# Attention units threaded between the pieces of a feed-forward pass: gates, keys and queries one place earlier, three result buffers, marked first loads, one guard on another engine

## The chip, the cores and the metric

One core of one Trainium2 chip (trn2). The time is the device time of one execution in microseconds; the kernel is run three times and the median is quoted. Beside the times there is one profiled execution, with a time and a span of its own; every row below comes from it.

## What is computed

A gated linear attention over 4 batches, 8 heads, 768 positions and head size 48, followed by a feed-forward pass on its output:

```
f = sigmoid(f_logit)
for t in range(768):
    state = f[t] * state + outer(k[t], v[t])      # per batch and head, 48 x 48
    y[t]  = q[t] @ state
x = y as (3072, 384)
out = (relu(x @ w_in) ** 2) @ w_out               # 384 -> 2048 -> 384
```

All data is float32. The feed-forward matmuls split each operand into a high part in the matmul's own type and a low part that is the difference, and use three matmuls for each product.

## The kernel before

**Blocks, units, pieces.** The 768 positions form six blocks of 128 (all four batches, so 512 columns). In each block the eight heads make four *units* of two heads, numbered through: unit n is block n // 4. The feed-forward pass of a block runs over 16 *pieces* f of 128 hidden rows (`Moe.run`, L175): `up` (L137) makes nine matmuls into a hidden buffer `ph` (two such buffers), `square` (L148) three ScalarE passes (relu, square, cast to `gh`), `rest` (L159) one VectorE subtraction that gives `gl` and frees the hidden buffer, and `down` (L165), two pieces later, nine matmuls into three accumulators `po`. `finish` (L201) copies the three accumulators to SBUF, on ScalarE, VectorE and ScalarE, and SyncE sends each out (L211).

**The steps of a unit** are letters (`Unit.stage`, L449): L, f, k, v load; G gates (L288, ScalarE sigmoid); K keys (L291, VectorE: a scan, a product, and a *guard*, L302, a maximum over 112x8 elements kept in `low`); Q queries (L304: a reciprocal of the guard's result, a scan, a product); T transposes on TensorE (L330), N their copy; D states and S scores on TensorE (L351, L362); M mask, C states on VectorE; r, s copies on ScalarE; Y outputs on TensorE (L400); H and X the high and low parts of the output (L425, L436); g copies of some rows between tiles by DMA (L440; on GpSimd's queue for blocks 0 and 1, on SyncE's after that).

**Weights** arrive as 64-bit words and are decoded on the chip (`decode`, L85), in four steps: an absolute value on ScalarE, four VectorE operations, a ScalarE cast that gives the high part, and a VectorE subtraction that gives the low part. There are 32 half weights (piece f, input or output matrix); a load is `weights_load` (L252), which can be *marked*: VectorE first writes one word of the destination (L256), so the load can't be issued before VectorE has come that far.

**What sets the order.** TensorE, SyncE, VectorE and ScalarE run their instructions in the order in which the program issues them; GpSimd's order is left to the scheduler. The prologue is written out by hand in `FIRST` and `SECOND` (L58, L64): a letter and a number are a step of a unit; i and o load a half weight, A I c J and B O d P are the four decode steps of an input and an output weight; `busy` are TensorE transposes without use; U R E W are `up`, `square`, `rest`, `down` of block 0. The prologue computes units 0 to 7, decodes ten half weights, and runs five pieces of block 0, whose sums are kept (`keep`, L191). After that the order of blocks is 1 (16 pieces), 0 (its other 11), then 2 to 5. In block 1 the other 22 half weights are decoded: piece n takes one where n is even and two where it is odd (n up to 14; L549). `before` (L557) runs the first two steps, and for the first of two also the cast, ahead of the piece; `after` (L563) the remaining steps, between `square` and `rest`. Weight loads for piece n are marked and issued at piece n - 4.

The units of blocks 2 to 5 are threaded into the pieces by two tables: unit i starts at piece `UNIT_AT[i]` (L55), counted over all blocks, and `STAGE_AT` (L52) lists its steps as (pieces later, place in the piece, letters). Place 0 is before `up`, 0.5 between `square` and `rest`, 1 after `down`. Its last steps, Y H X g, run at the start piece of the next unit, place 1. Units at 16, 27, 43 and 59 start at the first piece of a block; a block ends with two rounds of `down` alone and `finish`.

Of the kernel before, what the change touches and what calls it, by code (L numbers as in the profile page):

```python
# [12 lines left out]
F32 = mybir.dt.float32  # L13
# [4 lines left out]
ALU = mybir.AluOpType  # L18
ET = mybir.EngineType

P = 128
# [7 lines left out]
NT = B * TB  # L29
NZ = B * NC  # L30
CZ = C + 1
ROWS = 64 + D
# [16 lines left out]

STAGE_AT = ((-3, 0, "Lv"), (0, 0, "GK"), (0, 1, "TNQ"), (1, 1, "DSrMC"), (2, 1, "s"))  # L52


UNIT_AT = (13, 16, 18, 21, 24, 27, 31, 35, 39, 43, 47, 51, 55, 59, 63, 67, 71)  # L55


FIRST = """  # L58
f0 k0 v0 G0 L1 K0 v1 Q0 busy13 T0 L2 N0 D0 G1 r0 S0 C0 K1 s0 v2 i0 M0 busy4 T1 G2 Q1 Y0 o0 N1 L3 K2
r1 D1 H0 S1 A0 B0 X0 T2 M1 v3 N2 C1 D2 i1 Q2 s1 Y1 G3 o1 C2 r2 S2 K3 H1 L4 s2 A1 X1 busy2 T3 M2 g1  # L60
N3 Q3 Y2 v4 i2 D3 I0 H2 r3 S3 o2 G4 X2 c0 M3 L5 g2 C3 J0 s3 O0 B1 busy6 Y3 v5 K4 d0 i3 H3 G5 o3 X3
busy5 T4 P0 g3 N4 Q4 A2 D4 L6 C4 r4 busy3 S4 M4 s4 v6 I1 busy3 Y4 i4
"""
SECOND = """  # L64
U0 G6 O1 o4 H4 c1 X4 L7 R0 J1 K5 U1 d1 B2 v7 E0 T5 R1 P1 W0 Q5 N5 A3 D5 E1 r5 S5 C5 G7 W1 M5 s5 K6
Y5 Q6 H5 T6 N6 X5 r6 K7 D6 g5 S6 M6 T7 C6 N7 Q7 s6 Y6 I2 r7 H6 X6 c2 D7 g6 J2 S7 B3 C7 U2 M7 s7 O2
Y7 R2 I3 H7 d2 E2 c3 X7 P2 g7 J3 A4 W2 O3 B4 U3 I4 d3 P3 c4 R3 J4 O4 U4 E3 d4 R4 W3 P4 E4 W4
"""


class Moe:
# [103 lines left out]
    def run(self, hooks):  # L175
        for n in range(len(self.fs) + LAG):
            if n < len(self.fs):
                for hook in hooks.get((n, 0), ()):
                    hook()
                f = self.fs[n]  # L180
                self.up(f)
                self.square(f)
                for hook in hooks.get((n, 0.5), ()):
                    hook()
                self.rest(f)
            if n >= LAG:
                self.down(self.fs[n - LAG])
            for hook in hooks.get((n, 1), ()):
                hook()
# [11 lines left out]
    def finish(self, dst, part=None):  # L201
        nc = self.nc
        for e in range(NJ):
            if part:
                ob = part[e]
                nc.vector.tensor_tensor(out=ob, in0=self.po[e], in1=ob, op=ALU.add)
            else:
                tag = "ob" if self.blk == 1 else f"part{e}"
                ob = self.gp.tile([P, NT], F32, tag=tag, name=f"ob{self.blk}_{e}", bufs=1)
                (nc.vector.tensor_copy if e % 2 else nc.scalar.copy)(out=ob, in_=self.po[e])  # L210
            nc.sync.dma_start(dst(e), ob)  # L211

# [9 lines left out]
def fast_path(ctx, tc, moe, ident, low, fkqT, vN, w, out):  # L222
# [36 lines left out]
    class Unit:  # L259
# [31 lines left out]
        def keys(self):  # L291

            rr = self.wk([ROWS, NZ * CZ], "rr")
            V.tensor_tensor_scan(  # L294
                out=rr[:, ::-1], data0=self.fz[:, NZ * CZ : 0 : -1], data1=dr[:, ::-1], initial=0.0,
                op0=ALU.mult, op1=ALU.add,
            )
            V.tensor_tensor(  # L298
                out=chunks(self.kt), in0=chunks(self.kt), in1=scanned(rr)[:, :, 1:], op=ALU.mult
            )  # L300
            self.pe = low[:ROWS, self.n]
            V.tensor_scalar(out=self.pe, in0=rr[:, ::CZ], scalar1=LOWEST, scalar2=None, op0=ALU.max)  # L302

        def queries(self):  # L304

# [181 lines left out]
    def step(t):  # L487

        nm = t.rstrip("0123456789")
        n = int(t[len(nm) :])
        if nm == "busy":
            for _ in range(n):
                nc.tensor.transpose(out=pw[:, 0:P], in_=ident, identity=ident)
        elif nm in ("i", "o"):  # L500
            weights_load(n, "io".index(nm))
        elif nm in "AIcJBOdP":
            i = "AIcJBOdP".index(nm) // 4
            if nm in "AB":
                decoding[n, i] = moe.decode(n, i, pro)
            next(decoding[n, i])
        elif nm == "U":
            moe.up(n)
        elif nm == "R":
            moe.square(n)  # L510
        elif nm == "E":
            moe.rest(n)
        elif nm == "W":
            moe.down(n)
        else:
            unit(n).stage(nm)
# [3 lines left out]
    with tc.manual_schedule(engines={ET.PE, ET.SP, ET.DVE, ET.Activation}):  # L520
# [28 lines left out]
        for n in range(NF - 1):  # L549
            few = range(3 * n // 2, min(3 * (n + 1) // 2, len(halves)))  # L550
            for h in few:
                if n < AHEAD:
                    weights_load(*halves[h])
                else:
                    hook(0, n - AHEAD, 0.5, lambda h=h: weights_load(*halves[h], mark=True))

            def before(few=few):  # L557
                for h, last in zip(few, (None, *few)):
                    for m in (h, h, last):
                        if m is not None:  # L560
                            next(steps[m])

            def after(few=few):  # L563
                for h in few:
                    for _ in steps[h]:
                        pass

            hook(0, n, 0, before)
            hook(0, n, 0.5, after)
        hook(0, NF - 1, 0, third)  # L570
        for i in range(len(UNIT_AT) - 1):
            un = Unit(2 * HP + i, xs, (ps_a,))
# [182 lines left out]
```

## Time and profile before

| what | us |
|---|---|
| median of 3 runs (560.84 to 563.0) | 561.27 |
| the profiled execution | 561.55 |
| its span, first to last instruction | 559.8 |
| TensorE matmuls busy | 505.9 |
| VectorE busy | 302.1 |
| ScalarE busy | 277.3 |
| GpSimd busy | 7.3 |

In the profile PE is TensorE (PEld its weight loads), DVE VectorE, ACT ScalarE, POOL GpSimd and SP SyncE. A busy share is a mean over stages: the prologue (to about 96 us), block 1 with the decoding (to about 180 us), and the rest differ in what they wait for, so the profile is to be read stage by stage. In a row of the timeline the bracket at the end is the idle time of that engine just before, and what ended it; `issue` there, or as a link of the chain, is time in which an engine waited for nothing that the profile shows.

### The profile page before, as it was taken

The page shows a single profiled execution, that of the slowest core. Times are in us where ns is not written, and L with a number is a line of the kernel's source. Part 1 is how long each engine was busy: PE and PEld are TensorE (multiplying, and loading weights), DVE is VectorE, ACT ScalarE, POOL GpSimd, SP SyncE. Part 2 cuts the span into 40 slices and gives each one's busy share as a digit, 9 for nine tenths or more (in the row PEclk, how much of TensorE's full clock was granted, in tenths as well). Part 3 has the DMA queues.
Part 4 walks back from the last instruction along what each step waited for, and adds up shares of the span by engine and source line. Part 5 has one row for each costly group of instructions (what it writes and reads, how often), then busy time and mean ns, then how long its engine had stood idle before and what let it go on. Part 6 is the DMA issues. An engine that isn't in the chain of part 4 may idle for free.

```text
span 559.8 us, 11419 instructions
## 1 busy us (share of the span) xinstructions
PE 505.9 (90%) x4869; PEld 401.7 (72%) x4869; DVE 302.1 (54%) x571; ACT 277.3 (50%) x526; POOL 7.3 (1%) x23
## 2 busy tenths in 40 slices
PE   5758769898969699999999999999999999999994
PEld 4656556677747577777878878777877877788883
DVE  6967986788894565554453464444265442111110
ACT  3434545666654555545445455555355544444341
POOL 0101000000000000000000000000000000000000
PEclk9966869999989799999999999999999999999997
DMA  8999000234640332030220230221132000100001
GB/s 235 252 264 252 9 6 6 86 111 142 194 111 20 102 74 75 11 121 2 74 73 2 75 121 5 70 74 40 54 103 64 11 11 11 57 2 0 1 0 62
DMA packets 15066, 41.71 MB, mean 74 GB/s; under 512 B 2160, under 2 KB 5232, under 8 KB 15008
## 3 DMA queue, kind: packets, MB, share of 16 engines
q1 hardware_dynamic: 14624, 40.12, 25.9%
q0 software_dynamic: 384, 0.79, 0.8%
q8 instruction: 40, 0.66, 0.5%
q14 instruction: 18, 0.15, 0.1%
HBM read 33.82 MB, written 4.72 MB: 69 GB/s over the span
## 4 chain that ended last, share of the span: by engine, by line
PE 69%; DVE 16%; ACT 7%; issue 4%; DMA 2%; SPq 0%; DVEq 0%; ACTq 0%
PE po L170 30%; PE ph L144 29%; PE ds L367 2%; DVE wa L100 2%; DVE wa L103 2%; PE py L408 2%; PE ds L356 2%; ACT w L108 2%; DVE w L110 2%; DVE rr L308 2%; DMA fkq<-in_fkqT_dram 1%; PE py L420 1%; PE pk L334 1%; ACT gh L156 1%; ACT ph L155 1%
## 5 line engine op out<-in xcount | busy, mean ns | idle before, releaser
L144 PE MATMUL ph<-x,w 128*128 128x512 f32 x864 | 226.7, 408 | 7.7 <-DVE gl L161 7.0
L144 PEld LDWEIGHTS ph<-x,w 128*128 128x128 f32 x864 | 162.8, 193 | 49.6 <-DVE gl L161 8.1
L170 PE MATMUL po<-gh,w 128*128 128x512 f32 x576 | 181.3, 396 | 0.4 <-DVE w L110 0.4
L161 DVE TENSOR_TENSOR gl<-ph,gh 128x512 fp32r<-128x512 f32 x96 | 66.2, 690 | 168.4 <-ACT gh L156 168.4
L154 ACT ACTIVATE ph<-ph 128x512 f32<-128x512 f32 x96 | 55.9, 583 | 155.7 <-PE ph L144 155.6
L170 PEld LDWEIGHTS po<-gh,w 128*128 128x128 f32 x576 | 108.1, 188 | 26.7 <-DVE w L110 0.7
L170 PE MATMUL po<-gl,w 128*128 128x512 f32 x288 | 114.4, 397 | 2.2 <-ACT w L108 1.7
L170 PEld LDWEIGHTS po<-gl,w 128*128 128x128 f32 x288 | 54.2, 188 | 16.4 <-ACT w L108 1.8
L156 ACT CAST gh<-ph 128x512 fp32r<-128x512 f32 x96 | 56.4, 587 | 3.0
L155 ACT ACTIVATE ph<-ph 128x512 f32<-128x512 f32 x96 | 55.9, 582 | 3.0
L408 PEld LDWEIGHTS py<-sc,vn 64*64 64x64 f32 (+1 forms) x768 | 25.0, 141 | 15.1 <-issue 13.3
L408 PE MATMUL py<-sc,vn 64*64 64x64 f32 (+1 forms) x768 | 29.6, 242 | 6.6 <-issue 4.7
L294 DVE TENSOR_TENSOR_SCAN rr<-fz,dr 112x520 f32<-112x520 f32 x24 | 29.6, 1234 | 9.7 <-ACT fz L289 9.5
L420 PE MATMUL py<-rx,sx 48*48 48x64 f32 (+1 forms) x352 | 27.8, 231 | 2.8 <-issue 2.7
L308 DVE TENSOR_TENSOR_SCAN rr<-fz,dz 112x520 f32<-112x520 f32 x24 | 29.8, 1242 | 0.8
L108 ACT CAST w<-wa 128x384 fp32r<-128x384 f32 x32 | 16.4, 515 | 26.4 <-DVE wa L103 26.4
L334 PE MATMUL pk<-ident,fkq 112*128 112x112 f32 x96 | 16.7, 305 | 13.3 <-DVE fkq L298 11.0
L356 PEld LDWEIGHTS ds<-vn,kn 64*64 64x64 f32 (+1 forms) x768 | 16.9, 148 | 15.4 <-issue 5.0
L420 PE MATMUL py<-fkq,sp 48*48 48x64 f32 (+1 forms) x352 | 27.2, 231 | 0.0
L356 PE MATMUL ds<-vn,kn 64*64 64x48 f32 (+1 forms) x768 | 20.3, 239 | 7.5 <-issue 3.0
L420 PEld LDWEIGHTS py<-rx,sx 48*48 48x48 f32 (+1 forms) x352 | 23.8, 141 | 3.1 <-issue 2.9
L367 PE MATMUL ds<-fkq 48*64 48x64 f32 x768 | 22.1, 250 | 3.7 <-DVE fkq L311 2.8
(56 smaller groups left out, 368.7 us busy)
## 6 DMA issues: line engine op xcount, KB each, us to landing
fkq<-in_fkqT_dram SPq DMA_DIRECT2D x23, 672.0 KB, 6.1
raw<-in_w_dram SPq DMA_DIRECT2D x32, 384.0 KB, 9.1
vn<-in_vN_dram SPq DMA_DIRECT2D x24, 192.0 KB, 5.3
out_dram<-ob SPq DMA_DIRECT2D x15, 256.0 KB, 2.0
x<-ys SPq DMA_DIRECT2D x24, 64.0 KB, 2.3
x<-ys POOLq DMA_DIRECT2D x12, 64.0 KB, 6.4
out_dram<-part SPq DMA_DIRECT2D x3, 256.0 KB, 2.1
fkq<-in_fkqT_dram SPq DMA_DIRECT2D x1, 448.0 KB, 4.1
```

Of the source, the lines that this page charges most:

```text
L144: self.nc.tensor.matmul(self.ph[f], lhsT=l, rhs=r, start=j == 0 and i == 0, stop=j == NJ - 1 and i == 2)
L154: nc.scalar.activation(ph, ph, AF.Relu)
L155: nc.scalar.activation(ph, ph, AF.Square)
L156: nc.scalar.copy(out=gh, in_=ph)
L161: self.nc.vector.tensor_tensor(out=gl, in0=self.ph.pop(f), in1=gh.bitcast(F32), op=ALU.subtract)
L170: self.nc.tensor.matmul(self.po[e], lhsT=l, rhs=r, start=f == self.fs[0] and i == 0, stop=f == self.fs[-1] and i == 2,)
L294: V.tensor_tensor_scan(out=rr[:, ::-1], data0=self.fz[:, NZ * CZ : 0 : -1], data1=dr[:, ::-1], initial=0.0, op0=ALU.mult, op1=ALU.add,)
L308: V.tensor_tensor_scan(out=pp, data0=self.fz[:, : NZ * CZ], data1=dz, initial=0.0, op0=ALU.mult, op1=ALU.add)
L356: nc.tensor.matmul(self.ds[h * C : h * C + m, c, b * D : (b + 1) * D], lhsT=self.kn[rows, b, h * C : h * C + m], rhs=self.vn[rows, b, h * ...
L367: nc.tensor.matmul(self.ds[c * C : (c + 1) * C, h, B * D + b * C : B * D + (b + 1) * C], lhsT=self.kt[rows, cs], rhs=self.ra[rows, cs], st ...
L408: nc.tensor.matmul(self.py[h * C : h * C + m, c, b * C : (b + 1) * C], lhsT=self.vn[rows, b, h * D : h * D + m], rhs=self.sc[rows, h, b], ...
L420: nc.tensor.matmul(self.py[h * C : h * C + m, c, b * C : (b + 1) * C], lhsT=s[rows, b * D : b * D + m], rhs=q[rows], start=False, stop=b = ...
```

## The change

Six edits. `STAGE_AT` moves the loads from three to four pieces ahead, G and K from place 0 of a unit's first piece to place 1 of the piece before (which is directly ahead of that piece's other hooks, and at a block's first piece ahead of the last two `down` and of `finish`), and Q from after T, at place 1, to place 0.5, between `square` and `rest`. A new place 0.7 after `rest` takes the last weight's remaining steps, so that only the subtraction of the first of two stays ahead of `rest`. `finish` uses three different buffers for its three copies: `ob`, and one each of the rotating `gh` and `gl` buffers. The guard runs on GpSimd and is issued before the product instead of after it. The prologue's ten weight loads are marked. `FIRST` and `SECOND` list the same steps in a slightly different order, with five of the 36 `busy` transposes at other places, and with the weight loads i3, o3, i4 and o4 further back.

```diff
-STAGE_AT = ((-3, 0, "Lv"), (0, 0, "GK"), (0, 1, "TNQ"), (1, 1, "DSrMC"), (2, 1, "s"))
+STAGE_AT = ((-4, 0, "Lv"), (-1, 1, "GK"), (0, 0.5, "Q"), (0, 1, "TN"), (1, 1, "DSrMC"), (2, 1, "s"))
 FIRST = """
-f0 k0 v0 G0 L1 K0 v1 Q0 busy13 T0 L2 N0 D0 G1 r0 S0 C0 K1 s0 v2 i0 M0 busy4 T1 G2 Q1 Y0 o0 N1 L3 K2
-r1 D1 H0 S1 A0 B0 X0 T2 M1 v3 N2 C1 D2 i1 Q2 s1 Y1 G3 o1 C2 r2 S2 K3 H1 L4 s2 A1 X1 busy2 T3 M2 g1
-N3 Q3 Y2 v4 i2 D3 I0 H2 r3 S3 o2 G4 X2 c0 M3 L5 g2 C3 J0 s3 O0 B1 busy6 Y3 v5 K4 d0 i3 H3 G5 o3 X3
-busy5 T4 P0 g3 N4 Q4 A2 D4 L6 C4 r4 busy3 S4 M4 s4 v6 I1 busy3 Y4 i4
+f0 k0 v0 G0 L1 K0 v1 Q0 busy13 T0 L2 N0 D0 G1 S0 C0 r0 K1 s0 v2 i0 M0 busy4 T1 Q1 G2 Y0 o0 N1 K2 r1
+D1 L3 H0 S1 A0 X0 T2 B0 M1 C1 N2 v3 Q2 D2 s1 i1 Y1 G3 C2 o1 r2 K3 S2 s2 H1 L4 A1 X1 T3 M2 g1 N3 Q3
+Y2 v4 i2 D3 I0 H2 r3 S3 G4 X2 c0 M3 g2 C3 L5 J0 s3 O0 B1 busy6 Y3 o2 K4 d0 v5 H3 X3 busy5 T4 G5 P0
+g3 i3 N4 Q4 A2 busy3 D4 L6 C4 r4 busy2 S4 M4 s4 I1 busy3 Y4 v6
 SECOND = """
-U0 G6 O1 o4 H4 c1 X4 L7 R0 J1 K5 U1 d1 B2 v7 E0 T5 R1 P1 W0 Q5 N5 A3 D5 E1 r5 S5 C5 G7 W1 M5 s5 K6
-Y5 Q6 H5 T6 N6 X5 r6 K7 D6 g5 S6 M6 T7 C6 N7 Q7 s6 Y6 I2 r7 H6 X6 c2 D7 g6 J2 S7 B3 C7 U2 M7 s7 O2
+U0 H4 O1 c1 G6 X4 R0 J1 L7 K5 U1 d1 B2 E0 T5 R1 P1 W0 Q5 v7 N5 A3 D5 E1 r5 S5 C5 G7 W1 M5 s5 o3 K6
+Y5 Q6 T6 H5 N6 X5 r6 K7 D6 g5 S6 M6 T7 C6 N7 i4 o4 Q7 s6 Y6 I2 r7 H6 X6 c2 D7 g6 J2 S7 B3 C7 U2 M7
...
@@ Moe.run
                 self.rest(f)
+                for hook in hooks.get((n, 0.7), ()):
+                    hook()
@@ Moe.finish
-                tag = "ob" if self.blk == 1 else f"part{e}"
-                ob = self.gp.tile([P, NT], F32, tag=tag, name=f"ob{self.blk}_{e}", bufs=1)
+                tag, bufs = (("ob", 1), ("gh", None), ("gl", None))[e]
+                ob = self.gp.tile([P, NT], F32, tag=tag, name=f"ob{self.blk}_{e}", bufs=bufs)
@@ Unit.keys, after the scan
+            self.pe = low[:ROWS, self.n]
+            G.tensor_scalar(out=self.pe, in0=rr[:, ::CZ], scalar1=LOWEST, scalar2=None, op0=ALU.max)
             V.tensor_tensor(
                 out=chunks(self.kt), in0=chunks(self.kt), in1=scanned(rr)[:, :, 1:], op=ALU.mult
             )
-            self.pe = low[:ROWS, self.n]
-            V.tensor_scalar(out=self.pe, in0=rr[:, ::CZ], scalar1=LOWEST, scalar2=None, op0=ALU.max)
@@ step
-            weights_load(n, "io".index(nm))
+            weights_load(n, "io".index(nm), mark=True)
@@ hooks of the decoding
-            def after(few=few):
+            def after(few=few[:-1]):
                 for h in few:
+                    next(steps[h])
+
+            def last(few=few):
+                for h in few[-1:]:
                     for _ in steps[h]:
                         pass
             hook(0, n, 0, before)
             hook(0, n, 0.5, after)
+            hook(0, n, 0.7, last)
```

## Rows read from the trace of the kernel before

**Rows 1.** Table of stages: busy us (x instructions) of PE, PEld, DVE, ACT, POOL; clock; DMA.

```profile
98.00:154.00 56.00, 50.25 (x210) 38.60 (x208) 47.23 (x116) 36.49 (x73) 0.00 (x0) 1.00 0.44 134
154.00:172.00 18.00, 12.62 (x108) 9.60 (x107) 15.86 (x32) 10.24 (x21) 0.00 (x0) 0.91 0.37 85
172.00:194.00 22.00, 17.74 (x188) 13.99 (x187) 8.34 (x15) 8.44 (x16) 0.00 (x0) 0.84 0.25 77
...
240.00:480.00 240.00, 237.19 (x2387) 189.14 (x2387) 111.95 (x191) 122.01 (x229) 0.00 (x0) 1.00 0.19 53
```

**Rows 2.** Chain of waits in the first 100 us: start us, us, what.

```profile
26.49 4.04 issue
...
35.76 2.71 issue
```

**Rows 3.** VectorE's timeline in the prologue: start us, us, instruction, idle before.

```profile
32.32 0.69 DVE L438 TENSOR_TENSOR x<-py,x 112x512 fp32r<-112x512 f32 x1 [2.61 <-ACT x L434]
...
55.06 0.69 DVE L161 TENSOR_TENSOR gl<-ph,gh 128x512 fp32r<-128x512 f32 x1 [1.47 <-ACT gh L156]
```

**Rows 4.** DMA from 12 to 30 us: the total and one issue line.

```profile
DMA packets 1577, 4.74 MB, mean 264 GB/s; under 512 B 212, under 2 KB 493, under 8 KB 1575
...
x<-ys POOLq DMA_DIRECT2D x4, 64.0 KB, 8.7
```

**Rows 5.** DMA from 27 to 29 us, by queue: packets, MB, share.

```profile
q8 instruction: 1, 0.02, 4.0%
```

**Rows 6.** DMA from 56 to 98 us: one issue line.

```profile
x<-ys POOLq DMA_DIRECT2D x3, 64.0 KB, 2.1
```

**Rows 7.** Timeline of the decode stretch, VectorE and TensorE.

```profile
107.92 2.36 PE L144 MATMUL ph<-x,w 128*128 128x512 f32 x9 [1.31 <-DVE gl L161]
...
119.70 0.56 DVE L110 TENSOR_TENSOR w<-wa,w 128x384 fp32r<-128x384 f32 x1 [0.58 <-ACT w L108]
...
125.48 0.56 DVE L110 TENSOR_TENSOR w<-wa,w 128x384 fp32r<-128x384 f32 x1 [0.44 <-ACT w L108]
```

**Rows 8.** Timeline around block 2's first unit, TensorE.

```profile
154.99 2.33 PE L144 MATMUL ph<-x,w 128*128 128x512 f32 x9 [0.75 <-DVE gl L161]
...
164.06 0.60 PE L334 MATMUL pk<-ident,fkq 112*128 112x112 f32 x4 [4.63 <-DVE fkq L298]
...
164.43 3.89 PE L144 MATMUL ph<-x,w 128*128 128x512 f32 x9
...
171.44 2.36 PE L144 MATMUL ph<-x,w 128*128 128x512 f32 x9
```

**Rows 9.** Timeline of the seam of blocks 1 and 0, TensorE and ScalarE.

```profile
179.93 2.26 PE L144 MATMUL ph<-x,w 128*128 128x512 f32 x9
...
184.38 0.59 ACT L210 COPY ob<-po 128x512 f32<-128x512 f32 x1 [5.06 <-DMA out_dram<-ob]
...
188.24 4.07 PE L144 MATMUL ph<-x,w 128*128 128x512 f32 x9
...
193.34 2.37 PE L144 MATMUL ph<-x,w 128*128 128x512 f32 x9
```

**Rows 10.** TensorE's timeline at the seam before block 2.

```profile
252.32 0.69 PE L367 MATMUL ds<-fkq 48*64 48x64 f32 x32 [0.99 <-DVE fkq L311]
```

**Rows 11.** Chain of waits, one group of a steady piece.

```profile
259.51 2.10 PE po L170 x9
```

**Rows 12.** Groups by line and shape: busy us, mean ns, idle before.

```profile
L308 DVE TENSOR_TENSOR_SCAN rr<-fz,dz 112x520 f32<-112x520 f32 x24 | 29.8, 1242 | 0.8
...
L298 DVE TENSOR_TENSOR fkq<-fkq,rr 112x512 f32<-112x512 f32 x24 | 16.6, 692 | 0.8
...
L302 DVE TENSOR_SCALAR low<-rr 112x8 f32<-112x8 f32 x24 | 3.9, 164 | 0.0
...
L240 POOL TENSOR_SCALAR_AFFINE_SELECT mask<-mask 64x64 f32<-64x64 f32 x2 | 0.5, 234 | 0.1
```

**Rows 13.** The page's DMA issues: us from issue to landing.

```profile
out_dram<-ob SPq DMA_DIRECT2D x15, 256.0 KB, 2.0
```

More of the change, by code (lines that the diff above doesn't have):

```diff
@@ L48 @@
 ORDER = (3, 0, 1, 2)
-STAGE_AT = ((-3, 0, "Lv"), (0, 0, "GK"), (0, 1, "TNQ"), (1, 1, "DSrMC"), (2, 1, "s"))
+STAGE_AT = ((-4, 0, "Lv"), (-1, 1, "GK"), (0, 0.5, "Q"), (0, 1, "TN"), (1, 1, "DSrMC"), (2, 1, "s"))
 UNIT_AT = (13, 16, 18, 21, 24, 27, 31, 35, 39, 43, 47, 51, 55, 59, 63, 67, 71)
 FIRST = """
-f0 k0 v0 G0 L1 K0 v1 Q0 busy13 T0 L2 N0 D0 G1 r0 S0 C0 K1 s0 v2 i0 M0 busy4 T1 G2 Q1 Y0 o0 N1 L3 K2
-r1 D1 H0 S1 A0 B0 X0 T2 M1 v3 N2 C1 D2 i1 Q2 s1 Y1 G3 o1 C2 r2 S2 K3 H1 L4 s2 A1 X1 busy2 T3 M2 g1
-N3 Q3 Y2 v4 i2 D3 I0 H2 r3 S3 o2 G4 X2 c0 M3 L5 g2 C3 J0 s3 O0 B1 busy6 Y3 v5 K4 d0 i3 H3 G5 o3 X3
-busy5 T4 P0 g3 N4 Q4 A2 D4 L6 C4 r4 busy3 S4 M4 s4 v6 I1 busy3 Y4 i4
+f0 k0 v0 G0 L1 K0 v1 Q0 busy13 T0 L2 N0 D0 G1 S0 C0 r0 K1 s0 v2 i0 M0 busy4 T1 Q1 G2 Y0 o0 N1 K2 r1
+D1 L3 H0 S1 A0 X0 T2 B0 M1 C1 N2 v3 Q2 D2 s1 i1 Y1 G3 C2 o1 r2 K3 S2 s2 H1 L4 A1 X1 T3 M2 g1 N3 Q3
+Y2 v4 i2 D3 I0 H2 r3 S3 G4 X2 c0 M3 g2 C3 L5 J0 s3 O0 B1 busy6 Y3 o2 K4 d0 v5 H3 X3 busy5 T4 G5 P0
+g3 i3 N4 Q4 A2 busy3 D4 L6 C4 r4 busy2 S4 M4 s4 I1 busy3 Y4 v6
 """
 SECOND = """
-U0 G6 O1 o4 H4 c1 X4 L7 R0 J1 K5 U1 d1 B2 v7 E0 T5 R1 P1 W0 Q5 N5 A3 D5 E1 r5 S5 C5 G7 W1 M5 s5 K6
-Y5 Q6 H5 T6 N6 X5 r6 K7 D6 g5 S6 M6 T7 C6 N7 Q7 s6 Y6 I2 r7 H6 X6 c2 D7 g6 J2 S7 B3 C7 U2 M7 s7 O2
-Y7 R2 I3 H7 d2 E2 c3 X7 P2 g7 J3 A4 W2 O3 B4 U3 I4 d3 P3 c4 R3 J4 O4 U4 E3 d4 R4 W3 P4 E4 W4
+U0 H4 O1 c1 G6 X4 R0 J1 L7 K5 U1 d1 B2 E0 T5 R1 P1 W0 Q5 v7 N5 A3 D5 E1 r5 S5 C5 G7 W1 M5 s5 o3 K6
+Y5 Q6 T6 H5 N6 X5 r6 K7 D6 g5 S6 M6 T7 C6 N7 i4 o4 Q7 s6 Y6 I2 r7 H6 X6 c2 D7 g6 J2 S7 B3 C7 U2 M7
+s7 O2 Y7 R2 I3 H7 d2 E2 c3 X7 P2 g7 J3 A4 W2 O3 B4 U3 I4 d3 P3 c4 R3 J4 O4 U4 E3 d4 R4 W3 P4 E4 W4
 """
```

## Prediction, made before any run of the change

> **What bounds the kernel now.** I read the table of stages first, then the chain of waits stage by stage, then each engine's order of instructions around the links where the chain leaves TensorE. From 240 to 480 us TensorE is busy 237.2 of 240 us [rows 1]: a piece is two groups of nine matmuls of 2.10 us each [rows 11], 4.2 us, and only idle TensorE time can be won there. Three earlier stages are another matter: in 98:154 it idles 5.75 us, in 154:172 5.4 us, in 172:194 4.3 us, and in the last two the granted clock falls to means of 0.91 and 0.84 [rows 1]. Before 98 us look for what makes VectorE wait: there it runs almost without gaps.
>
> **Prologue (up to 96 us).** The chain has two links in which TensorE waits for nothing that the profile shows, 4.04 and 2.71 us, both within a unit's output matmuls [rows 2]. One packet of the instruction queue moves within 27 to 29 us [rows 5]: I take the first link for TensorE's instructions arriving late, and the second for the same. VectorE pays: it waits 2.61 us for the cast behind the first link [rows 3]. A 64 KB transfer between two tiles, issued on another queue, lands in a median of 8.7 us in this stretch [rows 4] and in 2.1 us after 56 us, with the engines nearly idle [rows 6]; so a small transfer loses about 6.6 us to the full queues. The change gives ten weight loads a marker written by VectorE, so SyncE can't issue them, nor any load behind them, until VectorE gets there. My sum: without the first link the cast comes before VectorE has finished the four decode operations ahead of it, so the 2.61 us go. Without the second the next such cast comes in time too; I count 0.9 us, a third of the link. The first hidden-layer group follows the last of these outputs, where VectorE waits 1.47 us for its cast [rows 3]; I count 0.7 us, half of it. Together 4.2 us. It can be 0 (the instructions still come late) or, with second link and last wait in full, 2.6 + 2.7 + 1.5 = 6.8 us.
>
> The held-back loads put waits on SyncE. Behind the first two markers is the fourth unit's 672 KB load. The second marker is written after the second unit's queries, some 16 us in; weights and load are 1056 KB, at the 264 GB/s of rows 4 some 4 us, and with the 2.1 us of a quiet small transfer they land near 22 us. VectorE wants that unit's gates at 22.5 us. I count 0; the ends are 0 and 4 us, should the load take the 8.7 us of the crowded queue. The marker is a memset of one word; bounded by the guard's 164 ns [rows 12], ten cost 0 to 1.6 us of VectorE. I take 0.6.
>
> **Guard on GpSimd.** It removes 24 instructions of 164 ns from VectorE [rows 12]; the next instruction starts before such a one has ended, so I count 0.07 us each, 0.6 us in the prologue's eight, which pays for the markers. GpSimd has no such instruction in the trace; its nearest row is a select of 64x64 elements at 234 ns [rows 12]. The guard starts beside the product of 692 ns that follows the scan, and would end before it; so 0. Only two units ask for queries straight after keys (the first, which then waits for a load anyway, and the seventh). Ends: 0 and, for the nine units of the stretches that VectorE bounds, 0.3 us each, 2.7 us. GpSimd's queue also holds the tile-to-tile transfers of the first two blocks, which wait for a unit's lower part; VectorE's order puts that part ahead of every guard written after it, so no guard waits for a later VectorE step. *The Trainium skill speaks against this edit*: GPSIMD Engine Reference, Key points, says that GpSimd shares its SBUF interfaces with VectorE and contends with VectorE instructions that have two SBUF inputs. The product is one. By that rule the guard would end after the product and the sum come out up to 2.7 us higher; no row here has the two engines side by side.
>
> **Decode stretch of block 1 (97 to 155 us).** Two pieces carry three weight decodes. Five such periods lie between the up-projections at 107.92 [rows 7] and 154.99 us [rows 8], 9.41 us each. In each, VectorE waits 0.58 and 0.44 us for ScalarE's cast of a weight [rows 7], and TensorE starts an up-projection late (1.31 us the first time [rows 7]) because `rest`, which frees its buffer, stands behind the last weight's subtraction. The edit puts `rest` ahead. Then VectorE does `rest` while ScalarE makes the cast, and both waits go: 9.41 - 1.02 = 8.39 us for VectorE, 8.4 for TensorE's four groups. Two engines at the same load don't mesh perfectly: I take 8.47, a gain of 0.94 per period, 4.7 us. The up-projection at 107.92 itself starts about its 1.31 us earlier by the same swap. Together 6.0 us; ends 0 and the 5.75 us idle plus a quarter microsecond of restart per period, 7.0.
>
> **First unit of block 2 (155 to 180 us).** Keys stand behind eight weight operations and TensorE waits 4.63 us for their product at its transposes; the next nine matmuls then take 3.89 us instead of about 2.1 [rows 8]: the clock is at its lower level, 1.2 GHz, after that wait. Now gates and keys come before piece 13's decodes, and queries between them and `rest`. VectorE stays the limit. From `rest` of piece 11 to that of piece 13 it has three decodes with subtractions, two `rest`, keys and queries. The first two items are one period's 8.4 us; keys and queries are each a scan of 1.24 and a product of 0.69 [rows 12], with a reciprocal of about 0.2: 4.1 us, so 12.5 us; and since up-projection 15 also needs the last subtraction, 13.2 us. Before, the distance was 16.45 us (154.99 to 171.44 [rows 8]). Gain 3.3 us; ends 1.5 (clock loss stays) and 5.5 (TensorE's own 10 us and one wait). TensorE's idle time there is cut in two smaller pieces.
>
> **Seam of blocks 1 and 0 (180 to 193 us).** All three result copies use one buffer, so ScalarE waits 5.06 us for transfers to land [rows 9], VectorE likewise, and behind ScalarE's wait stand the next unit's gates, then its keys, then TensorE's transposes: 4.26 us idle [rows 1], and the next nine matmuls take 4.07 us [rows 9]. Three buffers remove both waits, and gates and keys come before the copies as well. From the first up-projection (179.93) to the third (193.34) [rows 9] are 13.4 us; without waits there remain 3.4 us to the end of the previous unit's outputs, transposes 0.6 [rows 8], the second up-projection 2.1, state and score matmuls about 1.1: 7.2. Gain 6.2 us, ends 4.3 and 6.5. The borrowed `gh` and `gl` buffers are wanted again by the third piece of the next block, at least 4.2 us later, when a result has landed (2.0 us [rows 13]); if that cover failed, it would cost some 2 us at each seam.
>
> **Seams of later blocks.** Three times scores wait for queries, 0.99 us the first time [rows 10], and restart with 2.37 instead of 2.10 us for nine matmuls [rows 9, 11]; in 240:480 the idle time is 2.8 us [rows 1]. Queries now precede `rest` of the piece before, with ScalarE's three passes as cover: 2.8 + 3 x 0.27 = 3.6 us; ends 2 and 3.6. What waits behind them is that `rest`, wanted only two pieces on. In the steady pieces these moves cost 0. Loads go out four pieces ahead instead of three, so SyncE issues each one piece earlier and the cover before the gates grows to four pieces of 4.2 us.
>
> **Sum.** 4.2 + 6.0 + 3.3 + 6.2 + 3.6 = 23.3, less 0.3 for small things left over: 23.0 us. The profiled execution took 561.55 us (span 559.8 and 1.75 around it), 0.28 above the median of 561.27. Forecast 538.5 us.
>
> **Rivals.** *Holding loads back gives nothing* (the two links are not late instructions, or the loads only crowd the next ones): 542.7 us. For it: the profile names no cause at either link; against: the packet in the same stretch, and 8.7 against 2.1 us. The Trainium skill, Runtime: NRT & Kernel Launch, Instruction fetch mechanics, has the next block of instructions fetched while the current one executes, at a cost mostly hidden; by that rule this rival holds. *The decode stretch keeps its period*, because another in-order wait takes the place (ScalarE's weight cast ahead of its own relu): 544.5 us. Against it: ScalarE is busy 36.5 of 56 us [rows 1]. *The guard contends* and doesn't leave VectorE alone, so that part of the change doesn't do what it says: 541.2 us. *Slower*: held-back loads become the prologue's limit. Five units' loads stand behind markers; if each took 8.7 us or more and, with weights ahead of it, came 5 us after its cover ends, 25 us, that would make 563.5 us. It decides itself at the fourth unit's gates: if they run after 27 us rather than near 22, this is under way. Against: most of what crowds the queue is what is being held back.
>
> **Chances.** Forecast 0.58, no gain from loads 0.16, decode period kept 0.13, contention 0.06, slower 0.04, and 0.03 that gains and losses cancel. A measurement of this kernel can't tell less than about 0.5% (2.8 us) from no change: faster 0.93, same 0.03, slower 0.04. Range: upward to the decode rival with 2.5 us of another part missing, 547; downward, prologue (2.6 more), first unit (2.2 more) and decode (1.0 more) at their ends, not quite all at once: 533.5.
>
> **What would show it.** In the profile after: no idle TensorE time over 2 us between 25 and 40 us; a decode period near 8.5 us with no VectorE wait for a weight cast; no 4 us idle where 164 and 187 us were, and a granted clock of 1.00 there; results copied without waiting for a transfer; scores at later seams not waiting for queries. I am wrong if the period stays at 9.4 us, or if ScalarE's gates wait for loads beyond the third unit.

## The result and the profile after

The changed kernel takes 536.09 us (median of four executions, 535.00 to 538.29) against 561.13 us (four, 560.84 to 563.00): ratio 0.955, 95% interval 0.951 to 0.959. The forecast was 538.5 us with a range from 533.5 to 547. The profiled execution is the slowest of the four, 538.29 us with a span of 536.6.

The table of stages of the kernel after, columns as in [rows 1]:

```profile
98.00:154.00 56.00, 53.80 (x232) 42.50 (x231) 52.98 (x126) 39.21 (x78) 0.99 (x1) 1.00 0.51 161
154.00:172.00 18.00, 17.20 (x193) 13.43 (x192) 15.41 (x29) 12.53 (x25) 0.74 (x1) 1.00 0.12 45
172.00:194.00 22.00, 21.92 (x272) 17.41 (x271) 14.05 (x24) 13.96 (x28) 1.11 (x2) 1.00 0.35 88
240.00:480.00 240.00, 239.47 (x2280) 191.41 (x2280) 103.55 (x168) 122.19 (x227) 7.40 (x10) 1.00 0.17 46
```

The idle TensorE time of the four stretches fell from 5.75, 5.4, 4.3 and 2.8 us to 2.2, 0.8, 0.1 and 0.5, and the granted clock is 1.00 in all four. In 98:154 VectorE is now busy 52.98 of 56 us and TensorE 53.80. From piece 4 to piece 13 TensorE sets the pace: it has no idle time between 105 and 147 us, and its up-projections start every 4.20 us ((147.01 - 109.22) / 9), the time of a steady piece. VectorE's own period is only just shorter (experiment 9).

TensorE's timeline of the kernel after (answers to [rows 7 to 9]; start, duration, instruction, idle before):

```profile
94.64 4.36 PE L144 MATMUL ph<-x,w 128*128 128x512 f32 x18
...
104.93 2.36 PE L144 MATMUL ph<-x,w 128*128 128x512 f32 x9 [0.93 <-DVE gl L161]
...
109.22 2.26 PE L144 MATMUL ph<-x,w 128*128 128x512 f32 x9
...
147.01 2.26 PE L144 MATMUL ph<-x,w 128*128 128x512 f32 x9
...
152.12 0.60 PE L336 MATMUL pk<-ident,fkq 112*128 112x112 f32 x4 [0.74 <-DVE fkq L302]
152.49 2.34 PE L144 MATMUL ph<-x,w 128*128 128x512 f32 x9
...
158.41 0.69 PE L369 MATMUL ds<-fkq 48*64 48x64 f32 x32 [0.59 <-DVE fkq L313]
159.03 2.58 PE L144 MATMUL ph<-x,w 128*128 128x512 f32 x9
...
167.75 2.26 PE L144 MATMUL ph<-x,w 128*128 128x512 f32 x9
...
171.40 2.36 PE L144 MATMUL ph<-x,w 128*128 128x512 f32 x9
...
174.78 1.43 PE L144 MATMUL ph<-x,w 128*128 128x512 f32 x5
```

These are up-projections: block 1 begins at 94.64 (pieces 0 and 1 in one row), piece 3 starts at 104.93, piece 4 at 109.22, piece 13 at 147.01, piece 15 at 159.03, the next block's first three at 167.75, 171.40 and 174.78 (the last row ends with the view, after five of its nine). The waits of 4.63 us ahead of the first unit's transposes [rows 8] and of 5.06 us ahead of the result copy [rows 9] are gone. From these starts and those of before (block 1 began there at 96.35) the ledger of the two profiled executions, in us:

| stretch | before | after | gain | predicted |
|---|---|---|---|---|
| up to block 1's first product | 96.35 | 94.64 | 1.7 | 4.2 |
| to up-projection 13 (decode) | 58.64 | 52.37 | 6.3 | 6.0 |
| to up-projection 15 (first unit) | 16.45 | 12.02 | 4.4 | 3.3 |
| to the next block's first | 8.49 | 8.72 | -0.2 | 0 |
| to its third (seam) | 13.41 | 7.03 | 6.4 | 6.2 |
| to the end of the span | 366.46 | 361.82 | 4.6 | 3.6 |

It adds up to 23.2 us, against 23.3 less 0.3 predicted. The term that stands out is the first. VectorE's and ScalarE's timelines of the prologue after, and two links of its chain of waits:

```profile
25.86 1.24 DVE L296 TENSOR_TENSOR_SCAN rr<-fz,dr 112x520 f32<-112x520 f32 x1 [3.58 <-ACT fz L291]
...
53.25 0.69 DVE L161 TENSOR_TENSOR gl<-ph,gh 128x512 fp32r<-128x512 f32 x1 [0.81 <-ACT gh L156]
```

```profile
25.20 0.63 ACT L291 ACTIVATE fz<-fkq 112x512 f32<-112x512 f32 x1 [4.88 <-DMA fkq<-in_fkqT_dram]
```

```profile
15.62 0.33 SPq L259
...
16.00 9.18 DMA fkq<-in_fkqT_dram
```

Both TensorE links without a cause [rows 2] are gone, and so is the VectorE wait of 2.61 us [rows 3]. In their place VectorE waits 3.58 us for the fourth unit's gates: its load went out at 16.0 us, behind the markers, and landed 9.18 us later. TensorE's timeline of the same stretch:

```profile
27.93 0.98 PE L336 MATMUL pk<-ident,fkq 112*128 112x112 f32 x4 [4.41 <-DVE fkq L302]
...
39.21 0.60 PE L336 MATMUL pk<-ident,fkq 112*128 112x112 f32 x4 [2.52 <-DVE fkq L302]
```

TensorE idles 4.41 and 2.52 us for the keys of the fourth and the fifth unit. So here the prediction's sign of being right, no idle TensorE time over 2 us between 25 and 40 us, did not come, and its sign of being wrong, gates that wait for loads beyond the third unit, did: ScalarE waits 4.88 us.

Last, the guard, in the groups by line and shape of the kernel after, beside the product it runs with:

```profile
L301 POOL TENSOR_SCALAR low<-rr 112x8 f32<-112x8 f32 x24 | 17.8, 742 | 360.3 <-DVE rr L296 360.3
```

```profile
L302 DVE TENSOR_TENSOR fkq<-fkq,rr 112x512 f32<-112x512 f32 x24 | 16.6, 692 | 0.8
```

On GpSimd the guard takes 742 ns, not the 234 ns of the nearest row; the product beside it keeps the 692 ns of before [rows 12].

### The profile page after: what moved, and what is told of

It reads as the page before. It is cut to its first block, busy times and chain, and to the rows that moved or that the text cites. A ratio compares the mean times of both kernels' runs of the same rounds, so it can differ in the third digit from the quotient of the medians.

```text
span 536.6 us, 11462 instructions
## 1 busy us (share of the span) xinstructions
PE 498.2 (93%) x4869; PEld 397.7 (74%) x4869; DVE 299.0 (56%) x557; ACT 277.3 (52%) x526; POOL 25.4 (5%) x47
## 4 chain that ended last, share of the span: by engine, by line
PE 72%; DVE 16%; ACT 5%; DMA 3%; issue 2%; SPq 0%; ACTq 0%; DVEq 0%
PE po L170 31%; PE ph L144 31%; DMA fkq<-in_fkqT_dram 3%; DVE wa L100 2%; PE ds L369 2%; PE ds L358 2%; PE py L410 2%; DVE w L110 2%; DVE gl L161 2%; DVE wa L103 2%; PE pk L336 2%; PE py L422 2%; DVE wa L99 2%; DVE rr L310 1%; ACT w L108 1%
## 5 line engine op out<-in xcount | busy, mean ns | idle before, releaser
L144 PE MATMUL ph<-x,w 128*128 128x512 f32 x864 | 223.4, 404 | 2.6 <-DVE gl L161 2.0
L301 POOL TENSOR_SCALAR low<-rr 112x8 f32<-112x8 f32 x24 | 17.8, 742 | 360.3 <-DVE rr L296 360.3
L410 PEld LDWEIGHTS py<-sc,vn 64*48 64x48 f32 (+1 forms) x768 | 24.9, 142 | 10.1 <-issue 8.3
```

The lines of the kernel that those rows point to most:

```text
L144: self.nc.tensor.matmul(self.ph[f], lhsT=l, rhs=r, start=j == 0 and i == 0, stop=j == NJ - 1 and i == 2)
L410: nc.tensor.matmul(self.py[h * C : h * C + m, c, b * C : (b + 1) * C], lhsT=self.vn[rows, b, h * D : h * D + m], rhs=self.sc[rows, h, b], ...
```

## The experiments

A single execution is read by two lengths: the start of block 1, and the **rest**, from there to the end of the span. The rest repeats: 441.96 us in the profile above, 441.86 us in the second profile of the same kernel. The table gives for each kernel the fourth unit's gates on ScalarE (the start of that sigmoid), the two lengths, and the device time: a median of four or five executions, or one execution where "(1)" stands.

| kernel | gates | block 1 | rest | us |
|---|---|---|---|---|
| before | 20.01 | 96.35 | 463.45 | 561.13 |
| after | 25.20 | 94.64 | 441.96 | 536.09 |
| after again | 22.12 | 91.34 | 441.86 | 534.86 (1) |
| without markers | 19.59 | 96.73 | 443.07 | 537.92 |
| fourth load early | 19.86 | 93.08 | 442.02 | 534.37 |
| `rest` last | 21.82 | 90.91 | 450.89 | 543.54 (1) |
| one copy buffer | 21.57 | 90.26 | 445.54 | 537.46 (1) |
| old places | 24.75 | 93.81 | 450.79 | 546.35 (1) |
| queries late | 21.74 | 90.08 | 447.62 | 539.39 (1) |
| guard on VectorE, 32 B more | 21.75 | 91.36 | 433.54 | 526.48 |
| 32 B more | 21.58 | 93.14 | 433.96 | 528.65 |
| before, 32 B more | 19.93 | 95.79 | 456.11 | 552.87 |
| guard on VectorE, 64 B more | | | | 535.16 |
| the three put together, 96 B more | 20.15 | 91.13 | 436.87 | 528.78 |

**1. The markers.** Taken from all ten loads of the prologue:

```diff
-            weights_load(n, "io".index(nm), mark=True)
+            weights_load(n, "io".index(nm))
```

> The changed kernel with the prologue's ten weight loads unmarked again; order of the lists as changed. Theory (the markers took TensorE's late instructions away, and cost the fourth unit's gates a 3.58 us wait for their load): waits without a shown cause of about 4 and 2.7 us come back on TensorE between 20 and 40 us, VectorE no longer waits for the fourth unit's gates, the first up-projection of block 1 starts near 96 us instead of 94.6; some 1.5 us slower than the changed kernel, about 537.6. Rival (the new order of the lists did it, the markers only cost): no such waits, the 3.58 us gone, start near 91 us, about 532.5 us.

537.92 us (ratio to before 0.959, interval 0.955 to 0.963, which overlaps that of the change). TensorE's timeline and then VectorE's:

```profile
30.64 0.40 PE L410 MATMUL py<-sc,vn 64*48 64x64 f32 x4 [3.96 <-issue]
```

```profile
32.42 0.69 DVE L440 TENSOR_TENSOR x<-py,x 112x512 fp32r<-112x512 f32 x1 [3.02 <-ACT x L436]
...
54.90 0.69 DVE L161 TENSOR_TENSOR gl<-ph,gh 128x512 fp32r<-128x512 f32 x1 [2.33 <-ACT gh L156]
```

The first link is back with its old size (4.04 us before) and so are the VectorE waits behind it. The DMA view of this kernel from 27 to 31 us, its total and the instruction queue:

```profile
DMA packets 217, 0.88 MB, mean 220 GB/s; under 512 B 20, under 2 KB 26, under 8 KB 216
...
q8 instruction: 1, 0.02, 2.1%
```

The queues are full during the link (SyncE's transfers alone take 95.8% of the DMA engines' time), and one packet of instructions moves, as in [rows 5]. The fourth unit's wait is gone. So the link comes of loads that go out early, and the markers do remove it: it is also there, 3.77 us, in experiment 9's kernel before, while the longest TensorE wait of that kind between 15 and 42 us in a profile with markers is 1.70 us (experiment 3). The new order of the lists alone gains nothing: without markers block 1 starts at 96.73 us (96.35 before). The second link stayed away: that one was not shown to be the markers'. In time the exchange is worth 2.1 us of block 1's start here (96.73 against 94.64) and 5.4 us against the second profile below. By the Trainium skill (Runtime: NRT & Kernel Launch, Instruction fetch mechanics) fetching is mostly hidden; at this link, if it is a fetch, it was not: 3.96 us.

**2. The fourth unit's load** put ahead of the two markers:

```diff
-... K1 s0 v2 i0 M0 busy4 T1 Q1 G2 Y0 o0 N1 K2 r1
-D1 L3 H0 ...
+... K1 s0 v2 L3 i0 M0 busy4 T1 Q1 G2 Y0 o0 N1 K2 r1
+D1 H0 ...
```

> The changed kernel with the fourth unit's load of gates, keys and queries moved ahead of the first marked weight load. Theory (that load waits only because SyncE is held by two markers in front of it, and then lands 9.2 us after issue): it lands before 17 us, VectorE's wait of 3.58 us goes, no long wait of TensorE comes back; block 1 starts near 91.2 us, about 532.8 us. Rival (the instructions come late again, as the queue is full to 17 us): a TensorE wait of 2 us or more with no shown cause between 20 and 30 us, block 1 at 93.5 us or later, 535 or more.

534.37 us (ratio 0.953, interval 0.949 to 0.956). The 3.58 us wait is gone, and block 1 begins 1.6 us earlier, not 3.4: TensorE and VectorE now wait elsewhere. Against the second profile of the kernel after (experiment 3) it even begins 1.7 us later, so the move is not shown to win; the median is 1.7 us lower, with intervals that overlap. TensorE's timeline here, VectorE's, ScalarE's, and a link of the chain of waits:

```profile
33.00 0.36 PE L422 MATMUL py<-rx,sx 48*64 48x64 f32 x1 [2.06 <-ACT sx L330]
```

```profile
32.59 0.56 DVE L110 TENSOR_TENSOR w<-wa,w 128x384 fp32r<-128x384 f32 x1 [1.63 <-ACT w L108]
```

```profile
31.52 0.63 ACT L291 ACTIVATE fz<-fkq 112x512 f32<-112x512 f32 x1 [3.29 <-DMA fkq<-in_fkqT_dram]
```

```profile
22.65 8.85 DMA fkq<-in_fkqT_dram
```

The next load behind the markers takes the place of the first: the fifth unit's goes out at 22.65 us and lands 8.85 us later, ScalarE waits 3.29 us for it, and the copy and the cast that TensorE and VectorE wait for stand behind that unit's gates in ScalarE's order. The theory had only the fourth unit's load in view; the rival's wait without a shown cause did not come either.

**3. The changed kernel once more**, one profile:

> The changed kernel once more, for one profile of another execution. Theory: the landing of the fourth unit's load behind its two markers differs between executions of one program (9.18 us after its issue in the profile shown, 5.71 and 5.91 us in the two experiments that leave this stretch alone); if it lands in under 6.5 us here, VectorE's 3.58 us wait for that unit's gates is gone, the second block starts at 90 to 91.5 us in place of 94.64, and the time is 534 to 536 us. Rival: the nine microseconds belong to this kernel's own order of issues: then the wait of 3 to 4 us is there again and the block starts near 94.6.

The link of its chain of waits:

```profile
15.68 6.41 DMA fkq<-in_fkqT_dram
```

The load lands 6.41 us after its issue, VectorE's wait shrinks from 3.58 to 0.82 us, and block 1 begins at 91.34. In the experiments that keep this stretch it took 5.71 us (`rest` last), 5.91 (one copy buffer), 5.87 (32 B more) and 8.41 (old places). The landing differs between executions of one order of issues; the profile after had the longest one. In these eight profiles with markers ahead of the load block 1 begins between 90.08 and 94.64 us, median 91.35: 5.0 us earlier than before. Where the fourth unit's gates come in time, 2 to 3 us of spread remain (93.14 with 32 B more); most of it is the fifth unit's load again, in the chain of waits of that kernel:

```profile
22.89 9.20 DMA fkq<-in_fkqT_dram
```

There ScalarE waits 3.62 us for it and starts the fifth unit's gates at 32.12. In the five other profiles whose fourth gates start by 22.2 us, the fifth start between 29.66 and 30.97 and block 1 between 90.08 and 91.36.

**4. `rest` behind the last weight again.** The cast and subtraction of the last weight go back ahead of `rest`; all else stays:

```diff
-            def after(few=few[:-1]):
+            def after(few=few):
                 for h in few:
-                    next(steps[h])
+                    for _ in steps[h]:
+                        pass
...
             hook(0, n, 0.5, after)
-            hook(0, n, 0.7, last)
```

> The changed kernel with the last weight's cast and subtraction ahead of rest again. Theory (that order alone set the decode period): the period from one up-projection to the second after it is 9.4 us again instead of 8.42, VectorE waits for ScalarE's weight cast; five periods 4.9 us and the first 1.1: some 6 us slower than the changed kernel, about 542 us. Rival (earlier gates and queries, or the lighter VectorE without guards, made the stretch faster): period under 8.8 us, less than 2.5 us slower.

The rest is 8.9 us longer, where the theory had some 6. VectorE waits for ScalarE's cast of a weight again, 0.44 and 0.58 us in every period; in the kernel after it has no such wait between 98 and 154 us. TensorE's timeline:

```profile
102.51 2.36 PE L144 MATMUL ph<-x,w 128*128 128x512 f32 x9 [1.35 <-DVE gl L161]
...
149.58 2.34 PE L144 MATMUL ph<-x,w 128*128 128x512 f32 x9 [0.74 <-DVE gl L161]
...
162.29 0.69 PE L369 MATMUL ds<-fkq 48*64 48x64 f32 x32 [1.59 <-DVE fkq L313]
162.92 3.73 PE L144 MATMUL ph<-x,w 128*128 128x512 f32 x9
```

The period is that of before, (149.58 - 102.51) / 5 = 9.41 us, and from block 1's start to up-projection 13 are 58.67 us: the whole decode gain (6.3) hangs on this edit. What the theory left out is the next stretch: 13.34 us to piece 15 in place of 12.02, then 3.73 us for nine matmuls and another 1.3 us lost.

**5. One copy buffer again:**

```diff
-                tag, bufs = (("ob", 1), ("gh", None), ("gl", None))[e]
+                tag, bufs = ("ob" if self.blk == 1 else f"part{e}"), 1
```

> The changed kernel with the result copies in the old buffers (one for block 1). Theory (early gates and keys free TensorE's transposes, buffers free ScalarE's passes): ScalarE waits about 5 us again at the seam of blocks 1 and 0, but the transposes don't; from the first to the third up-projection about 9 us instead of 7.0 (13.4 before), 2 us slower than the changed kernel, 538. Rival (the buffers are the whole of it): 13 us again and a clock at its lower level, 6 us slower, 542.

The rest is 3.6 us longer, 3.0 of it at the seam: its first three up-projections start at 163.34, 167.00 and 173.40, 10.06 us against 7.03 (13.41 before). ScalarE's timeline and TensorE's:

```profile
167.79 0.59 ACT L212 COPY ob<-po 128x512 f32<-128x512 f32 x1 [5.06 <-DVE fkq L313]
```

```profile
171.52 0.88 PE L358 MATMUL ds<-vn,kn 64*64 64x48 f32 x29 [2.17 <-ACT ph L154]
```

ScalarE loses its 5.06 us at the copy again (the releaser named had long been done; with one buffer it is again the transfer out of it that comes last), but the gates and keys are already past. With the new order of steps the buffers are worth 3.0 us at the seam (the theory had 2) and 0.6 us after it.

**6. All old places** of a unit's steps, with the marker, the buffers and the place of `rest` kept:

```diff
-STAGE_AT = ((-4, 0, "Lv"), (-1, 1, "GK"), (0, 0.5, "Q"), (0, 1, "TN"), ...
+STAGE_AT = ((-3, 0, "Lv"), (0, 0, "GK"), (0, 1, "TNQ"), ...
```

> The changed kernel with the whole old list of places (gates, keys and queries back where they stood); marker, three buffers, order of the rest and GpSimd guard stay. Theory: each early move pays at its own place. The first unit's keys product again follows one piece behind its gates, so its [rows 8] wait of some 4.6 us is back and the stretch from the last decode gate product to the next piece goes from 12.02 us to 15 to 16.5; the seam goes from 7.03 us to about 8; each of the three later seams loses 1.3 us to a waiting score product [rows 10]. Together 7.8 to 9.6 us from the start of the second block to the end, stage by stage, against the changed kernel. Rival: once the rest comes with its 0.7 hook and the copies have their buffers, the old places hide as well; then at most 3 us over the same stages.

The rest is 8.8 us longer: 4.1 at the first unit, 1.2 at the seam, 3.8 after it, 0.2 won between. TensorE's timeline:

```profile
154.91 0.80 PE L336 MATMUL pk<-ident,fkq 112*128 112x112 f32 x4 [4.36 <-DVE fkq L302]
155.38 3.79 PE L144 MATMUL ph<-x,w 128*128 128x512 f32 x9
```

The stall of [rows 8] is back, with its slow products.

**7. The queries alone** back at place 1, gates and keys still early:

```diff
-... (-1, 1, "GK"), (0, 0.5, "Q"), (0, 1, "TN"), ...
+... (-1, 1, "GK"), (0, 1, "TNQ"), ...
```

> The changed kernel with the queries alone put back on the piece's end; gates and keys stay one piece early. Theory: the gain at the later seams came from the queries' half piece (the score products no longer wait for the query copy): score products wait again some 1.0 to 1.3 us at each of three later seams and about 1 us at the first one, 4 to 6 us in all from the second block's start. Rival: the early keys made that gain; then the seams stay within 1 us of the changed kernel's and no score product waits.

The rest is 5.7 us longer: 1.1 at the first unit, 1.2 at the seam, 3.5 after it, 0.2 won between. TensorE's timeline at the first two seams:

```profile
171.75 0.69 PE L369 MATMUL ds<-fkq 48*64 48x64 f32 x32 [0.99 <-DVE fkq L313]
...
231.37 0.69 PE L369 MATMUL ds<-fkq 48*64 48x64 f32 x32 [0.99 <-DVE fkq L313]
```

The waits of [rows 10] return (0.98 us each at the other two later seams), so the gain at the later seams is the queries'; early gates and keys give the 3.0 us more at the first unit.

Experiments 4, 5 and 6 summed lengthen the rest by 8.9 + 3.6 + 8.8 = 21.3 us; the change shortened it by 463.45 - 441.96 = 21.5. Each was taken out alone, and the three together come to nearly all of it. The loads' fourth piece of lead was only taken back together with the places (experiment 6) and has no price of its own.

**8. The guard back on VectorE,** and three of the same instruction alone on GpSimd at the start (they only add work):

```diff
+    alone = pers.tile([ROWS, NZ], F32, name="alone")
+    for _ in range(3):
+        G.tensor_scalar(out=alone, in0=dr[:, ::CZ], scalar1=LOWEST, scalar2=None, op0=ALU.max)
...
-            self.pe = low[:ROWS, self.n]
-            G.tensor_scalar(out=self.pe, in0=rr[:, ::CZ], scalar1=LOWEST, scalar2=None, op0=ALU.max)
             V.tensor_tensor(
                 out=chunks(self.kt), in0=chunks(self.kt), in1=scanned(rr)[:, :, 1:], op=ALU.mult
             )
+            self.pe = low[:ROWS, self.n]
+            V.tensor_scalar(out=self.pe, in0=rr[:, ::CZ], scalar1=LOWEST, scalar2=None, op0=ALU.max)
```

> The changed kernel with the guard back on VectorE behind the product, and three extra instructions on GpSimd, of the guard's own operation and shape, at the start, before VectorE has its first two-input product. Theory (contention): beside the products the guard took 742 ns on GpSimd; alone it takes 0.2 to 0.3 us, and on VectorE 164 ns [rows 12] 24 times, which adds some 3.9 us of VectorE time that lies mostly beside the matrix products: time within 0.7 us of the changed kernel's. Rival (own cost): GpSimd takes about 0.7 us for it alone too. Second rival, for the time: the guard's 742 ns beside the product was on the path, and the kernel gains over 1 us with VectorE's guard.

The three, in the groups by line and shape of this kernel:

```profile
L255 POOL TENSOR_SCALAR alone<-dr 112x8 f32<-112x8 f32 x3 | 0.7, 236 | 0.3
```

Alone, on another tile (`dr`), it takes 236 ns, beside the product 742. That agrees with the rule of the Trainium skill that was weighed (GPSIMD Engine Reference, Key points), and GpSimd is the one that waits: the product's 692 ns did not change. But the time fell to 526.48 us (ratio 0.939, interval 0.936 to 0.942), where neither theory had it: my theory said the time of the change, and the second rival, a gain of over 1 us with no size, put it down to the guard. The groups show where from. TensorE's products of the kernel after, and then of this one:

```profile
L170 PE MATMUL po<-gh,w 128*128 128x512 f32 x576 | 181.3, 396 | 0.4 <-DVE w L110 0.4
```

```profile
L170 PE MATMUL po<-gh,w 128*128 128x512 f32 x576 | 177.4, 389 | 0.5 <-DVE w L110 0.5
```

Each product is 7 ns shorter at the same granted clock. The edit had also put a new 32-byte tile ahead of the working pools. In the built program the first input tile stands at byte 168,032 of a partition in the kernels before and after, 32 past a multiple of 64, and at 168,064 here; likewise all inputs and all `gh` and `gl`, the operands that stream through these products. The decoded weights stand at the same addresses in all these kernels. Three more kernels separate guard and address; each adds this line, a tile of 32 bytes without use, to the kernel after, to the kernel before (9) and to the kernel of experiment 8 (10):

```diff
+    pad = pers.tile([ROWS, NZ], F32, name="pad")
```

**9. The 32 bytes alone,** in the kernel after and in the kernel before:

> The changed kernel, guard on GpSimd, with one unused tile of 32 bytes per partition ahead of the working pools and nothing else. Theory (address): it moves the matrix products' moving operands (inputs x, squares gh and gl) from addresses that leave 32 when divided by 64 to addresses that leave 0; a 128x512 product of the layer takes 389 ns in the trace in place of 396, and the last steady stretch holds 134 products in 30 us in place of 130. Some 76 pieces of 18 products each lie in the stretch that TensorE bounds: 76 x 18 x 7 ns = 9.6 us less, 525 us. Rival (guard): the experiment with the guard back on VectorE won its 8.4 us because GpSimd no longer works beside VectorE; then the pad does nothing here and the time is 534 to 537 us.

> The kernel before with the same unused 32 bytes and nothing else. Theory (address): it has the same stretch of some 76 pieces, so it gains about 9 us: 550 to 553 us, products of 389 ns in the trace. Rival: its products stay at 396 ns and the time within 1 us of 560.6.

528.65 us (ratio 0.942, interval 0.938 to 0.945) and 552.87 us (0.985, 0.979 to 0.991). TensorE's up-projections in a steady stretch, of the kernel after and of the kernel after with 32 B more:

```profile
487.30 2.26 PE L144 MATMUL ph<-x,w 128*128 128x512 f32 x9
491.50 2.26 PE L144 MATMUL ph<-x,w 128*128 128x512 f32 x9
495.70 2.26 PE L144 MATMUL ph<-x,w 128*128 128x512 f32 x9
```

```profile
486.94 2.20 PE L144 MATMUL ph<-x,w 128*128 128x512 f32 x9
491.02 2.20 PE L144 MATMUL ph<-x,w 128*128 128x512 f32 x9
495.10 2.20 PE L144 MATMUL ph<-x,w 128*128 128x512 f32 x9
```

A piece takes 4.08 us in place of 4.20, 6.7 ns for each of its 18 products. The rest is 8.0 us shorter than that of after, and 7.3 us in the kernel before. The theory's 9.6 us counted the decode stretch as TensorE's; there the gain is small. Up-projections 3 and 13 of the kernel after with 32 B more:

```profile
103.37 2.35 PE L144 MATMUL ph<-x,w 128*128 128x512 f32 x9 [0.98 <-DVE gl L161]
...
145.13 2.34 PE L144 MATMUL ph<-x,w 128*128 128x512 f32 x9
```

A period takes (145.13 - 103.37) / 5 = 8.35 us in place of 8.42, where two of TensorE's pieces would take 8.16: here VectorE is the limit.

**10. The guard's place alone,** experiment 8 with a pad that restores the remainder of 32:

> The experiment with the guard back on VectorE, with another 32 bytes beside its own, so that the moving operands stand at the changed kernel's remainders of 32 again. Theory (address): this is then the guard's place alone; GpSimd's 742 ns lay beside other work and VectorE's 164 ns do too: 534 to 536.5 us and products of 396 ns. Rival (guard): the time stays near 526.5 us with the guard on VectorE, whatever the addresses.

535.16 us (ratio 0.956, interval 0.952 to 0.960), by times alone: the execution that was profiled took 2,657 us, the other four 533.87 to 538.12, and no row of that profile is used, so its products' 396 ns are not checked. With the operands where they were, the guard's place makes no difference that can be measured. With them moved, the rests differ by 0.4 us (433.54 and 433.96); the medians differ by 2.2 us, with intervals that overlap, and block 1 starts 1.8 us apart in the two profiles.

**11. Put together:** experiment 2's early load, the guard on VectorE, and a pad of 96 bytes (`ROWS, 3 * NZ`):

> The changed kernel with an unused tile of 96 bytes (the moving operands' addresses then leave 0 when divided by 64, but 64 when divided by 128), the fourth unit's load issued ahead of the markers, and the guard on VectorE. Theory: a remainder of 0 by 64 is what the products need: 389 ns each, 434 us from the second block's first product to the end of the span, and with that block starting at 91 to 93 us a time of 526 to 528 us. Rival: they need 0 by 128: then 396 ns, 442 us and 533 to 536 us.

528.78 us (ratio 0.946, interval 0.942 to 0.950), between the two theories. The steady stretch:

```profile
487.31 2.22 PE L144 MATMUL ph<-x,w 128*128 128x512 f32 x9
491.43 2.22 PE L144 MATMUL ph<-x,w 128*128 128x512 f32 x9
495.55 2.22 PE L144 MATMUL ph<-x,w 128*128 128x512 f32 x9
```

A piece takes 4.12 us, so a remainder of 0 by 64 with 64 by 128 gives most of it, and 0 by 128 the rest. Block 1 starts at 91.13 us here and at 93.08 in experiment 2, with the same order of loads; the fifth unit's gates start at 30.74 and 31.52. The best version measured is the kernel of experiment 8, 526.48 us.

## Why the prediction was right, step by step

The total was right, 536.1 for 538.5 us, and the terms behind block 1's start hold one by one. That the ledger's 23.2 us meet the forecast's 23.0 so closely is luck: 2.5 us missing in the prologue are made up by 2.1 us more at the first unit and the later seams.

- **Decode: right.** Predicted period 8.47 us, measured (147.01 - 104.93) / 5 = 8.42; VectorE no longer waits for a weight's cast. The two limits of the sum, 8.39 us for VectorE and 8.4 for TensorE, were right too: TensorE takes 8.40 from piece 4 on, VectorE 8.35 where TensorE is faster (experiment 9). The allowance for engines that don't mesh wasn't needed. Experiment 4 gives the 6.3 us back in full. The rival that the period stays is out.
- **First unit: right mechanism, undersized.** 4.4 us for 3.3. The sum counted 13.2 us for VectorE between two up-projections; it took 12.02; which item was too large is not shown. The stall shrank to 0.74 and 0.59 us, and the clock stayed at 1.00.
- **Seam: right,** 6.4 us for 6.2. From 13.41 us, buffers with the old places come to 8.23 (experiment 6), the new places with one buffer to 10.06 (experiment 5), both to 7.03: either takes away part of the same wait, the buffers the larger one.
- **Later seams: undersized,** 4.6 for 3.6 us. The queries' place is 3.5 of it by experiment 7, the predicted term; in the profile after no score product waits at a later seam. What was left out are the copy buffers, 0.6 us after the seam by experiment 5, and early gates and keys, 3.8 - 3.5 = 0.3 by experiments 6 and 7.
- **Prologue: the step that was off** is "I count 0" for the fourth unit's load. It was to land near 22 us; in the profiled execution the gates ran at 25.2, within the end of 4 us that was given, and the term came out at 1.7 us in place of 4.2. In six of the eight profiles with that order they ran between 21.6 and 22.1, and over all eight the median gain is 5.0 us. ScalarE waited for that load in all eight (1.2 to 4.9 us), which is the prediction's own sign of being wrong, and in most of them for the fifth unit's as well (up to 3.6 us), which the sum did not look at. The slower rival's mark (fourth gates after 27 us) was never reached, but its mechanism, loads held back too long, is at work at both units. That the markers remove the first link was right (experiment 1); for the second link, which I took for the same, it is not shown.
- **Guard: the price was wrong, the cost right.** 0 on the path was right, 234 ns and "would end before the product" were wrong. The rival that it contends is half true as a mechanism: the guard takes 742 against 236 ns, but VectorE is left alone, its product keeping 692 ns. In time it is worth nothing that can be measured (experiment 10), not 2.7 us; that the guard's result is seldom wanted at once fits this, but no run tests it.

What the prediction never asked was what a steady piece is made of. It took 4.2 us a piece as fixed; 0.12 us of it was the address of the operands, worth 7 to 8 us here, nearly a third of what the whole change won.

## What to carry to other kernels

Hold a load back only if what stands behind it in the same queue has slack for the slowest landing seen, not for the mean rate: one order of issues gave 5.7 to 9.2 us for the same 672 KB. When one such wait is cured, look at the next load behind the same kind of marker: here it took the first one's place. Put an instruction that frees a buffer ahead of work whose result is wanted only later, and give a result copy its own buffer: at the seam here that was worth more than moving the steps. When a kernel's time changes with an edit that should do nothing, compare the duration of one steady instruction first: here 389 against 396 ns showed it at once, and one unused tile of 32 bytes gave 7.4 us (536.09 to 528.65).

## What the runs showed of the hardware

- A 128x512 product of the layer costs 226.7 ns of TensorE's time (4.08 us / 18) where the streamed operands' addresses are multiples of 128 bytes, 228.9 ns (4.12) where they leave 64 when divided by 128, and 233.3 ns (4.20) where they leave 32 when divided by 64, all at a granted clock of 1.00. Only the pool's place was moved, so inputs, squares and the units' tiles moved together and the weights stayed; which of them counts, and why, is open.
- A maximum over 112x8 elements on GpSimd took 742 ns beside a VectorE product with two SBUF inputs and 236 ns without one; that VectorE product took 692 ns with the guard beside it and without.
- With the DMA queues full, TensorE waited 3.77, 3.96 and 4.04 us for nothing that the profile names, at one place in three kernels; when the ten weight loads of the prologue are held back, the wait is gone. That it is the fetching of its instructions fits the one packet of the instruction queue there, but no run shows the packet ending the wait.
